# Issuing the first expert's output stores from ScalarE instead of SyncE

## The chip, the cores and the metric

The kernel runs on one core of a Trainium2 chip. The metric is the device time of one launch, in microseconds (us). Before the change it is 1227.88 us, the median of three runs (1226.94 to 1229.16).

## What is computed

The reference chains three blocks in fp32:

```python
scores = scale * np.matmul(q, k.transpose(0, 1, 3, 2))     # 4 x 8 heads, 576 x 576, head width 64
kth = np.partition(scores, -32, axis=-1)[..., -32:-31]     # the 32nd largest of each row
scores = np.where(scores >= kth, scores, -1e9)
attn = softmax(scores);  x = attn @ v                      # 2304 tokens x 512
g = x @ w_gate;  x = (silu(g) * (x @ w_val)) @ w_out       # first expert, inner width 1536
h = x @ w_in;    out = (h * np.cos(h)) @ w_out             # second expert, inner width 2048
```

## The kernel before

**Tiling.** The 2304 tokens are 18 tiles of 128. They are worked through in ten chunks: two of one tile, then eight of two tiles. For each chunk, each of four head pairs, each tile and each head there is one unit of attention (144 in all): TensorE makes the scores in PSUM (L591 or L598), ScalarE copies them to SBUF (L603), VectorE finds the 32 largest with four MAX8 (L628) and three MATCH_REPLACE8 (L631), ScalarE makes the masked exponentials (L659, L670), TensorE transposes them (L692), ScalarE fetches the transposed blocks (L698) and TensorE multiplies with V (L745, L748). In between run the matmuls of the first expert of the chunk before: gate and value (L903), with ScalarE fetching from PSUM (L869, L870, L881), GpSimd multiplying, ScalarE rounding the result (L965), and the output matmul (L1070), which sums a tile's output in one of two PSUM banks named y.

**The step that changes.** When a tile's output sum is finished, `y_proc` (L1092) turns it and writes it to the DRAM buffer y1, from which the second expert loads it (L1332). It does so in two halves of 256 columns, 36 halves in all. For each half ScalarE copies the sum to the SBUF tile yo (L1105), TensorE transposes its two 128x128 blocks back into the bank (L1111), ScalarE copies the transposed blocks into the same yo tile (L1116), and a DMA stores the tile, 128 KB, to y1 (L1117). There is one yo buffer (`r_yo` is a ring of one), so the copy L1105 of the next half waits until the store before it has landed. The bank is free for the next tile after the second half's copy.

**Queues and order.** The program is laid out ahead of time by a small planner (`Plan`, L90): every step is a generator item with an engine, a planned cost and a due time, the planner runs the items in planned time, and each item's function appends its instructions to the engines' queues at that moment. On the chip every engine then runs its own queue strictly in order and waits on semaphores. A DMA stands in the queue of the engine that issues it. Before the change all DMAs but two at the very start (L465) are issued by SyncE (SP): the output weights of the first expert (wo; L376, L378, L380), raw second-expert weights (L357) and their converted form (L361), Q, K and V loads (L490, L515, L542, L544), the stores in question (L1117), the second expert's inputs and weights (L1332, L1247) and its stores (L1576, L1694). A store in SP's queue waits there for ScalarE's copy L1116, and every DMA behind it waits with it. The planner's item that holds the copy and the store is one ScalarE item of 0.27 us planned cost.

**The second expert.** After the attention the second expert runs as two long runs of matmuls: L1407 (input product, in seven products per 2x2 block scheme) and L1684 (output product), with VectorE and ScalarE splitting operands (L1374, L1378, L1290, L1293, L1655, L1659) and making h·cos(h) (L1544 to L1561).

Of the kernel before, what the change touches and what calls it, by code (L numbers as in the profile page):

```python
# [165 lines left out]
def topk_attention_moe_moe(ctx: ExitStack, tc: tile.TileContext, qT, kT, vP, w1, wo1, w2, out):  # L166
    nc = tc.nc
# [4 lines left out]
    y1 = dram.tile([128, KT, NTOK], F32, name="y1")  # L172
# [681 lines left out]
    def moe_due(c, f):  # L854
        return due_unit((FIRST[c] + SIZES[c]) * H) + 20.0 + f * SIZES[c] * H * PACE / NF1
# [236 lines left out]
    def y_proc(c, i):  # L1092
        due = moe_due(c, NF1) - 80.0 * (c >= NCH - 2)
        bank = yt[i % NYB]
        y4 = bank.rearrange("p (f n) -> p f n", f=KT)
        for half in range(2):
            ko = yo_count[0]
            yo_count[0] += 1
            yield r_yo.gate(ko)
            y2 = y4[:, 2 * half:2 * half + 2]  # L1100
            st = {}

            def fetch(y2=y2):
                st["y"] = moe.tile([128, 2, 128], F32, tag="yo", name="yo", bufs=r_yo.n)
                nc.scalar.activation(st["y"], y2, AF.Copy)  # L1105

            yield "ACT", 0.27, fetch, due, True

            def turn(y2=y2):
                for j in range(2):  # L1110
                    nc.tensor.transpose(y2[:, j], st["y"][:, j], ident)  # L1111

            yield "PE", 0.22, turn, due + 2.0, True

            def store(y2=y2, half=half):
                nc.scalar.activation(st["y"], y2, AF.Copy)  # L1116
                nc.sync.dma_start(y1[:, 2 * half:2 * half + 2, i * 128:i * 128 + 128], st["y"])  # L1117

            end = yield "ACT", 0.27, store, due, True
            r_yo.free(ko, end + 2.5, plan)  # L1120
        r_y[i % NYB].free(i // NYB, end, plan)
        ev_y1[i].set(end + 2.5, plan)
# [661 lines left out]
```

## Time and profile before

| what | value |
|---|---|
| median of three runs | 1227.88 us (1226.94 to 1229.16) |
| the profiled execution | 1223.17 us, of which 1221.4 us are the span of its instructions |
| TensorE (PE) busy | 1169.9 us, 96% |
| VectorE (DVE) busy | 1002.2 us, 82% |
| ScalarE (ACT) busy | 937.9 us, 77% |
| GpSimd (POOL) busy | 574.8 us, 47% |
| granted TensorE clock, mean | 0.993 of full speed |
| the DMAs that move | 36 stores of 128 KB, first issue at 166.3 us, last at 853.7 us |

How to read the profile: it is one execution of the program taken by the hardware profiler. An engine is busy while one of its compute instructions runs; issuing a DMA is not busy time. `SPq` or `ACTq` mark what an engine's sequencer does (issue a DMA, wait for an event). L1117 is line 1117 of the kernel. `y<-yo` means that the instruction writes the tensor y and reads the tile yo. Ahead of each wait stands the instruction that waited, behind the arrow what ended its wait. PEld is the weight load that goes ahead of a matmul. Engines overlap the tail of one instruction with the head of the next, so starts can lie closer together than durations.

### The profile page before, as it was taken

What the parts mean: (1) busy time and instruction counts of PE and PEld (TensorE: products, weight loads), DVE (VectorE), ACT (ScalarE), POOL (GpSimd) and SP (SyncE); (2) the same over time, 40 slices, a digit from 0 to 9 for tenths busy, and PEclk for the clock granted to TensorE, in tenths of its full rate; (3) what the DMA queues carried; (4) which work ended last, traced back from release to release, by engine and by line L of the source; (5) the groups of instructions that cost most, each with busy time, mean ns of one, the idle gap of its engine ahead of it and who ended that gap; (6) DMA issues with size and microseconds to landing.
All of it is one profiled execution on the core that took longest, in us unless ns stands there. A gap on an engine that the chain in (4) does not pass through costs nothing. (4 is left out here: it accounts for less than half of the span.)

```text
span 1221.4 us, 23299 instructions
## 1 busy us (share of the span) xinstructions
PE 1169.9 (96%) x7720; PEld 1018.3 (83%) x7720; DVE 1002.2 (82%) x1984; ACT 937.9 (77%) x2085; POOL 574.8 (47%) x1036
## 2 busy tenths in 40 slices
PE   5799979999999999999999999999999999999998
PEld 3577646898888898898988898999999998888887
DVE  7999999999999999999999997277867778644541
ACT  4789999898889989898988887446756678755651
POOL 4898976876687876777766765300000000000000
PEclk9799999999999999999999999999999999999999
DMA  7455556665545653656545533463344276443430
GB/s 260 152 189 169 178 159 195 205 205 184 191 152 165 226 176 123 210 181 202 179 150 187 175 121 102 158 215 124 124 166 136 110 249 199 147 122 104 129 104 27
DMA packets 138985, 199.96 MB, mean 164 GB/s; under 512 B 19312, under 2 KB 88432, under 8 KB 138864
## 3 DMA queue, kind: packets, MB, share of 16 engines
q1 hardware_dynamic: 138704, 198.40, 51.1%
q8 instruction: 61, 1.00, 0.3%
q14 instruction: 60, 0.49, 0.1%
q10 hardware_dynamic: 160, 0.07, 0.0%
HBM read 152.28 MB, written 46.14 MB: 162 GB/s over the span
## 5 line engine op out<-in xcount | busy, mean ns | idle before, releaser
L628 DVE MAX8 m<-w 128x8 f32<-128x576 f32 x432 | 309.5, 747 | 1.8
L903 PE MATMUL gv<-x,w 128*128 128x256 f32 x2016 | 271.2, 286 | 0.3 <-ACT hg L870 0.3
L903 PEld LDWEIGHTS gv<-x,w 128*128 128x128 f32 x2016 | 252.2, 191 | 2.9 <-ACT hg L870 0.9
L631 DVE MATCH_REPLACE8 w<-m,w 128x576 f32<-128x576 f32 x288 | 213.0, 742 | 0.0
L1684 PE MATMUL b<-w2o,gp 128*128 128x512 f32 x864 | 202.1, 396 | 0.0
L1684 PEld LDWEIGHTS b<-w2o,gp 128*128 128x128 f32 x864 | 162.4, 188 | 38.7
L1407 PE MATMUL b<-xc,w 128*128 128x288 f32 x1344 | 182.1, 297 | 2.2 <-DVE h L1472 2.2
L1407 PEld LDWEIGHTS b<-xc,w 128*128 128x128 f32 x1344 | 180.2, 189 | 3.3 <-DVE h L1472 2.7
L1070 PE MATMUL y<-wo,gh 128*128 128x512 f32 x400 | 147.1, 414 | 4.1 <-DMA wo<-wo 1.9
L659 ACT ACTIVATE e<-s,b 128x576 f32<-128x576 f32 x144 | 113.5, 789 | 9.8 <-POOL b L642 9.5
L628 DVE MAX8 m<-s 128x8 f32<-128x576 f32 x144 | 107.2, 745 | 12.8 <-ACT s L603 11.6
L670 ACT ACTIVATE e<-e,b 128x576 f32<-128x576 f32 x144 | 114.1, 793 | 4.2 <-POOL b L646 0.3
L603 ACT ACTIVATE s<-sc 128x576 f32<-128x576 f32 x144 | 95.0, 660 | 20.3 <-PE sc L591 16.2
L698 ACT ACTIVATE pt<-tp 128x512 f32<-128x512 f32 (+1 forms) x216 | 101.4, 498 | 11.3 <-PE tp L692 10.7
L631 DVE MATCH_REPLACE8 w<-m,s 128x576 f32<-128x576 f32 x144 | 106.9, 742 | 0.0
L692 PE MATMUL tp<-ident,e 128*128 128x128 f32 x648 | 98.3, 275 | 8.8 <-ACT e L670 3.6
L1070 PEld LDWEIGHTS y<-wo,gh 128*128 128x128 f32 x400 | 75.0, 189 | 26.2 <-issue 4.0
L598 PE MATMUL sc<-K,q 128*128 128x288 f32 (+1 forms) x512 | 92.1, 307 | 3.9 <-ACT s L603 3.6
L692 PEld LDWEIGHTS tp<-ident,e 128*128 128x128 f32 x648 | 77.7, 141 | 19.7 <-ACT pt L698 5.5
L1070 PE MATMUL y<-wo,gl 128*128 128x512 f32 x208 | 84.8, 414 | 3.8 <-POOL wo L249 3.5
L598 PEld LDWEIGHTS sc<-K,q 128*128 128x128 f32 (+1 forms) x512 | 73.4, 183 | 10.8 <-ACT s L603 5.8
L748 PE MATMUL av<-pt,V 128*64 128x256 f32 (+3 forms) x832 | 75.2, 324 | 0.0
(115 smaller groups left out, 2081.6 us busy)
## 6 DMA issues: line engine op xcount, KB each, us to landing
wo<-wo SPq DMA_DIRECT2D x96, 512.0 KB, 3.6
gr<-gd SPq DMA_DIRECT2D x72, 256.0 KB, 3.2
w_raw<-in_w SPq DMA_DIRECT2D x32, 511.8 KB, 4.5
V<-in_vP SPq DMA_DIRECT2D x52, 256.0 KB, 3.0
w<-in_w SPq DMA_DIRECT2D x24, 511.5 KB, 5.7
kx<-in_kT SPq DMA_DIRECT2D x64, 144.0 KB, 3.0
wo<-wo SPq DMA_DIRECT2D x36, 256.0 KB, 3.0
gd<-h SPq DMA_DIRECT2D x32, 288.0 KB, 2.1
```

Source lines behind the costliest of these rows:

```text
L598: nc.tensor.matmul(sc[:r1, s, :HALF], q[:, a, (t - t0) * 128:(t - t0) * 128 + r1], k[:, s * HALF:s * HALF + HALF], start=a == 0, stop=a == 1)
L603: nc.scalar.activation(st["s"], sc[:, :, :HALF], AF.Copy)
L628: nc.vector.max(out=st["m"][:, 8 * i:8 * i + 8], in_=st["w"] if i else st["s"])
L631: nc.vector.match_replace(out=st["w"], in_to_replace=st["m"][:, 8 * i:8 * i + 8], in_values=st["w"] if i else st["s"], imm_value=LOWEST)
L659: nc.scalar.activation(st["e"], st["s"], AF.Prelu, bias=st["b"][:, 1:2], scale=SCALE, alpha=STEEP)
L670: nc.scalar.activation(st["e"], st["e"], AF.Exp, bias=st["b"][:, 2:3], scale=1.0, accum_out=smT[c, p, g][:, j:j + 1])
L692: nc.tensor.transpose(st["ps"][:, j - j0], e[:, j * 128:j * 128 + 128], ident)
L698: nc.scalar.activation(pt[:, j0:j1], st["ps"][:, :j1 - j0], AF.Copy)
L903: nc.tensor.matmul(gv[g], W1[f, kk // 2][:, a, g, kk % 2], m, start=kk == 0 and i == 0, stop=kk == KT - 1 and i == 2)
L1070: nc.tensor.matmul(bank, m, w, start=f == 0 and n == 0, stop=f == NF1 - 1 and n == len(terms) - 1)
L1407: nc.tensor.matmul(ps[b], w[:, a, side, kk], x[:, e, kk], start=start and kk == 0 and m == 0, stop=kk == 1 and m == 2, skip_group_check=True)
L1684: nc.tensor.matmul(st["o"], g[:, a, cs], W2O[f][:, b], start=f == 0 and i == 0, stop=f == NF2 - 1 and i == 2)
```

## The change

The DMA that stores a half of a tile's output is put in ScalarE's queue, directly behind the copy that fills its source, and no longer in SyncE's. Nothing else differs: the copy, the buffers, the planned costs and the order of all other instructions are the same.

```diff
             def store(y2=y2, half=half):
                 nc.scalar.activation(st["y"], y2, AF.Copy)
-                nc.sync.dma_start(y1[:, 2 * half:2 * half + 2, i * 128:i * 128 + 128], st["y"])
+                nc.scalar.dma_start(y1[:, 2 * half:2 * half + 2, i * 128:i * 128 + 128], st["y"])
 
             end = yield "ACT", 0.27, store, due, True
             r_yo.free(ko, end + 2.5, plan)
```

## Rows read from the trace of the kernel before

**Rows 1.** The page, part 1: busy time, share of the span, instructions.
```profile
span 1221.4 us, 23299 instructions
...
PE 1169.9 (96%) x7720; PEld 1018.3 (83%) x7720; DVE 1002.2 (82%) x1984; ACT 937.9 (77%) x2085; POOL 574.8 (47%) x1036
```

**Rows 2.** The chain that ended last, in order of time: start us, us, what.
```profile
853.21 10.50 PE b L1407 x78
...
882.36 132.26 PE b L1407 x990
...
1019.02 198.81 PE b L1684 x852
```

**Rows 3.** Busy us of each engine in the stretches that hold the stores.
```profile
core 0: us, PE busy (x) PEld busy (x) DVE busy (x) ACT busy (x) POOL busy (x), PEclk, DMA share, GB/s
160.00:210.00 50.00, 42.65 (x234) 29.09 (x235) 47.48 (x95) 45.61 (x105) 32.22 (x51) 0.97 0.59 178
285.00:308.00 23.00, 21.23 (x155) 18.34 (x153) 23.00 (x51) 20.59 (x53) 15.31 (x31) 1.00 0.47 142
373.00:397.00 24.00, 23.95 (x197) 22.39 (x197) 21.35 (x44) 23.40 (x62) 18.26 (x34) 1.00 0.47 143
458.00:483.00 25.00, 25.00 (x192) 23.01 (x191) 25.00 (x55) 24.56 (x64) 15.15 (x31) 1.00 0.33 99
534.00:560.00 26.00, 25.43 (x204) 22.95 (x201) 24.84 (x52) 23.93 (x61) 20.40 (x36) 1.00 0.56 174
620.00:648.00 28.00, 27.11 (x205) 24.77 (x204) 27.62 (x58) 25.30 (x65) 19.25 (x40) 1.00 0.53 163
700.00:728.00 28.00, 28.00 (x210) 25.38 (x207) 27.66 (x57) 23.02 (x62) 19.79 (x41) 1.00 0.37 115
780.00:800.00 20.00, 20.00 (x158) 19.50 (x157) 11.65 (x22) 11.17 (x26) 0.00 (x0) 1.00 0.61 195
835.00:856.00 21.00, 20.82 (x152) 20.24 (x152) 14.78 (x28) 15.41 (x32) 0.00 (x0) 1.00 0.34 108
```

**Rows 4.** The tile yo: duration ns min/median/max, first and last start, waits, landing.
```profile
L1105 ACT ACTIVATE yo<-y x36: 363/386/537, 164.6 to 851.0; 128x256 f32<-128x256 f32 x36
L1116 ACT ACTIVATE yo<-y x36: 361/386/507, 165.9 to 853.3; 128x256 f32<-128x256 f32 x36
L1117 SPq DMA_DIRECT2D y<-yo x36: 360/371/663, 166.3 to 853.7; - x36
...
DMA to landing us min/median/max: 1.8/1.9/3.8
```

**Rows 5.** Waits: of SP's queue at the stores; of the engines around them.
```profile
SPq L1117 <- ACT yo L1116: 56.8, 20, 5.5
...
PEld y L1111 <- ACT yo L1105: 5.8, 11, 1.1
...
ACT yo L1105 <- DMA y<-yo: 5.2, 6, 1.4
...
PE y L1111 <- ACT yo L1105: 2.7, 6, 0.9
```

**Rows 6.** ScalarE's timeline around one store: start us, us, instruction [idle before].
```profile
627.75 0.38 ACT L1116 ACTIVATE yo<-y 128x256 f32<-128x256 f32 x1
628.01 0.66 ACT L603 ACTIVATE s<-sc 128x576 f32<-128x576 f32 x1
...
632.04 0.38 ACT L1105 ACTIVATE yo<-y 128x256 f32<-128x256 f32 x1 [1.19 <-DMA y<-yo]
```

**Rows 7.** The line L465, issued by both queues at the program's start: ns min/median/max.
```profile
L465 SPq DMA_DIRECT2D qr<-in_qT x8: 465/570/1435, 3.1 to 17.9; - x8
L465 ACTq DMA_DIRECT2D qr<-in_qT x2: 547/627/707, 0.9 to 1.5; - x2
```

**Rows 8.** SP's timeline at the first stores, and the matmul that waits on SP's load.
```profile
163.76 1.29 SPq L515 DMA_DIRECT2D qx<-in_qT  x2
166.27 0.38 SPq L1117 DMA_DIRECT2D y<-yo  x1
166.75 5.10 SPq L376 DMA_DIRECT2D wo<-wo  x3
...
169.47 2.03 PE L1070 MATMUL y<-wo,xw 128*128 128x512 f32 x2 [2.33 <-DMA wo<-wo]
```

## The prediction

> **What bounds the kernel now.** I read the busy times first: TensorE is busy 1169.9 of 1221.4 us, ScalarE 937.9 [rows 1]. Busy time is only an average, so next comes the chain that ended last. From 882.36 us on it is nearly nothing but TensorE: 132.26 us of L1407 and 198.81 us of L1684 in one piece each, and before that a piece of 10.50 us from 853.21 [rows 2]. The last store is issued at 853.7 [rows 4]. So the last third of the kernel holds no store and runs at TensorE's pace; the change can only move the moment at which that third begins. Third, the stretches that hold the stores, seven of 23 to 50 us with four stores each between 160 and 728 us and two later ones with four each [rows 3]. From 373 us on the reader sees TensorE without slack there (23.95 of 24, 25.00 of 25, 25.43 of 26, 27.11 of 28, 28.00 of 28 us), VectorE hardly looser, and ScalarE, the engine that gets the new work, 23.40 of 24 and 24.56 of 25 us busy in two of them. Between 160 and 210 TensorE has room (42.65 of 50) and VectorE sets the pace (47.48). Last, the waits: SP stands 56.8 us in 20 waits at the stores for their copy, while the weight load of the transpose waits 11 times in 36 for ScalarE's copy L1105 [rows 5]. A copy that comes later still therefore meets a TensorE that is already waiting for it.
>
> **What is removed.** SP loses 36 issues at a median of 371 ns, 13.4 us [rows 4], and the waits at the stores [rows 5]. SP computes nothing, and its time counts only where a load behind a store is late and an engine waits for it. The clearest case: at 169.47 TensorE waits 2.33 us for a wo load that SP issued at 166.75, right behind the store of 166.27; the issue before that one ended at 163.76 + 1.29 = 165.05 [rows 8]. Freed of the store, the load could go out up to 166.27 - 165.05 = 1.2 us sooner. I take 0 of it: TensorE idles 7.35 us of those 50 us [rows 3] anyway, and VectorE, the nearer bound there, doesn't wait for this product. If that cover is not real it is a gain of 1.2 us.
>
> **What is added.** ScalarE runs in order. Today the instruction behind the copy starts 628.01 - 627.75 = 0.26 us after the copy's start, while the copy still runs [rows 6]. With the store behind it, the queue must first wait until yo is written (0.38 us), then issue the DMA, and only then pass on the next instruction. SP takes 0.371 us for the issue [rows 4]. ScalarE issuing this store is not in the trace; on the one line that both queues issue, ScalarE takes a median of 627 ns against SP's 570, 1.10 times as long [rows 7], so I take 0.41 us. The price of a store is then 0.38 + 0.41 - 0.26 = 0.53, with some 20 ns between copy and issue 0.55 us. Below it lies 0, if issuing held nothing up; above it 0.38 + 0.707 + 0.02 - 0.26 = 0.85 us with ScalarE's longest issue [rows 7]. I take 0.55, since the 371 ns are of this very transfer. In sum 36 x 0.55 = 19.8 us of ScalarE's queue.
>
> Queued behind the waiting store on ScalarE are the score copies (L603) that VectorE waits for, the fetches that free TensorE's banks (L698, L869, L870, L881) and the next L1105. The price is hidden where ScalarE would have idled before anyone misses its result. Four stores cost 4 x 0.55 = 2.2 us a stretch. ScalarE's idle time in the seven stretches is 4.39, 2.41, 0.60, 0.44, 2.07, 2.70 and 4.98 us [rows 3]. In four of them it covers the 2.2 us; in the other three it falls short by 1.60, 1.76 and 0.13, together 3.5 us. There ScalarE ends the stretch late, and as TensorE is 98 to 100% busy in these it has no idle time in which to catch up what it loses. In the two stretches after 780 us ScalarE idles 8.83 of 20 and 5.59 of 21 us, so the eight stores there cost 0; if that cover fails, 8 x 0.55 = 4.4 us. A count from the other side: TensorE's load already waits for L1105 in 11 transposes, and six L1105 themselves wait for a landing [rows 5], a wait that swallows the price of the store before; so 5 to 11 transposes are hit at 0.55 us, 2.8 to 6.1 us. The 3.5 lies within. With the price 0.85 the same subtraction gives shortfalls of 0.99, 2.80, 2.96, 1.33 and 0.70 us, 8.8 us; with the price 0 it gives 0.
>
> **The landing.** The next half's L1105 waits for the landing of the store before it in six cases, 5.2 us together, 1.19 of them at 632.04 [rows 5, 6]; a store lands 1.8 to 3.8 us after its issue, median 1.9 [rows 4]. The trace has no store of this kind on a queue of its own. Bounds: unchanged, or all 5.2 us gone; a slower landing, by the 0.04 us of the longer issue, is too small to count. I take unchanged, as the median is close to the minimum already. Beside it the Trainium skill, in the page "DMA: Bandwidth & Descriptors", section "Issuing engines are not separate DMA queues", says that transfers started by several engines share the same 16 DMA engines and that only the sequencer's issue time is saved, usually small beside the transfer. By that rule the landing is unchanged and the change saves no more than SP's issue time, which stands on no path here; it speaks against a gain.
>
> **The sum.** -0 (SP) + 3.5 (ScalarE) - 0 (landing) = +3.5 us: the profiled execution of 1223.17 us would become 1226.7. That execution lies 4.7 us below the median of the runs, 1227.88, so I put the difference on the median: 1231.4 us. About 0.2% (2.5 us) is what a measurement of this kernel can tell from no change.
>
> **Rivals.** *Hidden.* ScalarE's late 0.55 us never reaches TensorE, because what TensorE takes from it lies ready in the other buffers. For it: in the 458 to 483 stretch ScalarE idles only 0.44 us and yet TensorE is 25.00 of 25 us busy [rows 3], so it doesn't live from hand to mouth. Against it: the 11 waits for L1105 [rows 5]. Time: 1227.9.
>
> *Faster: the landing.* SP's loads are large, and a store that is queued behind one lands late; from ScalarE's own queue it need not. Its place is the wait of L1105 for the landing. It decides once those landings fall from up to 3.8 us to about the 1.8 of the fastest and so give back more than the new price takes. Worth: TensorE waited 2.7 us in all for L1105, ScalarE 5.2 [rows 5], so 2.7 to 5.2; with the price hidden, and 4 us taken between the two, 1223.9. Against it: only six of 36 copies waited so, and every one of the 36 stores pays. Beside it the same page, section "Queues, rings and completion order", says that each DMA engine goes round between the queue rows it has work for, packet by packet; by it a store would overtake loads that are queued on SP's row, which is this rival.
>
> *Heavy.* Every late microsecond stays, because each engine is kept busy by the one before: 19.8 us, 1247.7. For it: in the four stretches from 373 to 648 us TensorE, VectorE and ScalarE are all busy 89% or more [rows 3]. Against it: the idle time of ScalarE within the same rows, and the hold-up of at most 0.55 us at a time.
>
> **How the numbers follow.** The forecast (a part of the price reaches TensorE, 0 to +8.8 us, likeliest +3.5) gets 0.43, hidden 0.27, faster by the landing 0.18, heavy 0.12. The likeliest time is 1231.4. The range goes from 1224.5, which takes in hidden and the weaker half of the faster rival, to 1241, the forecast with its dearer price and the beginning of the heavy case; outside lie about 0.1 on each side. Slower by over 0.2%: heavy 0.12 and 0.38 of the forecast, 0.50. Within 0.2%: hidden, and the forecast's low end, 0.32. Faster: 0.18. The likeliest case's own range is 1228 to 1237.
>
> **What would show it.** In the profile after, the stores stand under ScalarE's queue, and the instruction behind a copy L1116 starts about 0.26 + 0.55 = 0.8 us after the copy's start; 0.26 again would mean no price, over 1.1 a dearer one. SP's waits at L1117 are gone; whether its time turns into earlier loads shows at the 2.33 us wait for wo. The wait of L1111 for L1105 grows from 2.7 us if the forecast holds and shrinks if the landing wins. ScalarE's wait for the landing, 5.2 us, should stay near its size less the price that it swallows; near 0 with landings all at 1.8 speaks for the faster rival. The long run of L1407, which began at 882.36, begins some 3.5 us later. The prediction is wrong if that run begins at the same time or sooner, or over 9 us later.

## The result and the profile after

| what | before | after |
|---|---|---|
| median of five runs each | 1227.88 us (1226.94 to 1229.16) | 1239.57 us (1238.24 to 1242.06) |
| ratio, 95% interval | | 1.0089 [1.0071, 1.0108]: slower |
| the profiled execution / its span | 1223.17 / 1221.4 us | 1238.24 / 1236.5 us |

The kernel got slower, by 0.9%, or 11.7 us between the medians. The forecast had the sign and 3.5 us. (The kernel before was run five times too; the table ahead of the prediction says three. The ratios here and below are the record's own and needn't equal the quotient of two medians; where a figure in us comes from a ratio, the text says so.) The two profiled executions lie 15.1 us apart, because the one of before is 4.7 us below its median; below, a position in one execution is read against a position in the same execution wherever it can be.

First the busy times of after (its page, part 1), the lines that answer to [rows 1]. No engine runs more instructions than before. Of the 15.1 us TensorE idles 9.6; its 7720 matmuls are also busy 5.5 us longer (1175.4 against 1169.9), of which some 1.9 are found in the tail, below, and the rest wasn't followed up.

```profile
span 1236.5 us, 23270 instructions
...
PE 1175.4 (95%) x7720; PEld 1019.9 (82%) x7720; DVE 1003.4 (81%) x1984; ACT 939.1 (76%) x2085; POOL 573.7 (46%) x1036
```

The chain that ended last (start us, us, what), against [rows 2]. The long piece of L1407 begins at 897.43, where before it began at 882.36: all 15.1 us are lost before it, and its own 132.27 us are as before. Two landings of stores now stand in the chain, at 791.63 and 805.05, where before there was one (2.62 us, at 791.38).

```profile
791.63 6.11 DMA y<-yo
...
805.05 3.03 DMA y<-yo
...
897.43 132.27 PE b L1407 x990
```

The tile yo of after, as in [rows 4]. The stores are in ScalarE's queue (ACTq), their issue takes 366 ns, and the slowest landing has gone from 3.8 to 6.1 us.

```profile
L1105 ACT ACTIVATE yo<-y x36: 362/386/425, 164.7 to 866.6; 128x256 f32<-128x256 f32 x36
L1116 ACT ACTIVATE yo<-y x36: 363/387/445, 165.9 to 868.5; 128x256 f32<-128x256 f32 x36
L1117 ACTq DMA_DIRECT2D y<-yo x36: 366/366/400, 166.4 to 868.9; - x36
...
DMA to landing us min/median/max: 1.8/2.1/6.1
```

The waits of after (sum us, times, longest). SP's line of 56.8 us at L1117 [rows 5] is gone. TensorE's waits for the copy L1105 have grown, 5.8 to 13.8 us for its weight load and 2.7 to 8.9 for its matmul; ScalarE's for a landing from 5.2 to 8.2. TensorE's longest single wait of each kind is about three times that of before.

```profile
PEld y L1111 <- ACT yo L1105: 13.8, 14, 3.0
...
PE y L1111 <- ACT yo L1105: 8.9, 12, 2.8
...
ACT yo L1105 <- DMA y<-yo: 8.2, 6, 3.8
```

ScalarE's timeline at one store (start us, us, instruction, [idle before it]), against [rows 6]. The next instruction, L603, starts 636.64 - 635.82 = 0.82 us after the copy, where before it was 0.26: the price of a store is 0.56 us here, and 0.55 to 0.68 at the others (next starts 0.81 to 0.94 after the copy's), but for one of 0.86; the mean of the next starts is 0.86, so the mean price 0.60. The trace itself says why: 0.44 us idle, ended by the copy whose end the store waited for, with the issue of 0.37 us in that gap.

```profile
635.82 0.38 ACT L1116 ACTIVATE yo<-y 128x256 f32<-128x256 f32 x1
636.23 0.37 ACTq L1117 DMA_DIRECT2D y<-yo  x1
636.64 0.65 ACT L603 ACTIVATE s<-sc 128x576 f32<-128x576 f32 x1 [0.44 <-ACT yo L1116]
```

**Where the time went.** Busy time of each engine from 20 to 780 us and from 780 to 815, of before and then of after; columns as in [rows 3]. By 780 us TensorE has done 5062 matmuls instead of 5116. The gap grows fastest behind that: in the 35 us that follow, 214 instead of 253, with 3.6 us of TensorE idle and the clock granted at 0.95, where before it was busy 34.73 of 35 us.

```profile
20.00:780.00 760.00, 723.29 (x5116) 620.70 (x5117) 716.77 (x1481) 661.78 (x1575) 569.10 (x1017) 0.99 0.55 173
780.00:815.00 35.00, 34.73 (x253) 32.84 (x252) 23.40 (x47) 16.55 (x38) 0.00 (x0) 1.00 0.72 236
```

```profile
20.00:780.00 760.00, 717.99 (x5062) 614.26 (x5063) 718.33 (x1481) 659.50 (x1566) 562.14 (x1009) 0.99 0.54 172
780.00:815.00 35.00, 31.36 (x214) 27.86 (x213) 12.01 (x23) 14.70 (x35) 5.82 (x9) 0.95 0.45 141
```

Store by store, the copy L1116 of after runs later than the same copy of before by 2.5 us at the fifth store, 3.2 at the 12th, 5.2 in the stretch of 458 us, 7 to 8.5 in that of 534, some 8 through the two after it, 9.3 at the 29th, 14.0 at the 32nd and 15.2 at the last. So there are two losses of different kinds: a slow one over 28 stores, and 4.7 us within three stores. How late one execution is by the 29th store says little about its size: e8 below, which is the kernel before up to there, is 5.3 us late at that store in its own execution. The slow loss is therefore taken from medians. From the 29th to the 32nd store that same execution loses 0.3 us, so a loss of 4.7 us over these three stands out.

The second, in lines. ScalarE and TensorE of after behind the 29th store: it is issued at 791.63, lands 6.11 us later, ScalarE stands 3.83 us for its buffer, and TensorE 2.78 us for ScalarE.

```profile
791.22 0.38 ACT L1116 ACTIVATE yo<-y 128x256 f32<-128x256 f32 x1 [2.02 <-PE y L1111]
791.63 0.37 ACTq L1117 DMA_DIRECT2D y<-yo  x1
...
797.76 0.38 ACT L1105 ACTIVATE yo<-y 128x256 f32<-128x256 f32 x1 [3.83 <-DMA y<-yo]
```

```profile
798.20 0.69 PE L1111 MATMUL y<-ident,yo 128*128 128x128 f32 x2 [2.78 <-ACT yo L1105]
```

The wait isn't all of the 4.7 us. Between the copies of the 29th and the 32nd store (columns as in [rows 3]; before, then after) TensorE idles 2.78 us and is busy 1.93 us longer, for nearly as many matmuls (126 on the trace against 123), and the clock granted is 0.91. After the wait it was 0.50, the lower of its two levels (1.2 GHz), from 798 to 800 us, 0.68 in the next 2 us and 1.00 from 802 on; a run of 36 matmuls of L903 that took 4.55 us before the wait (from 790.88) takes 5.78 behind it (from 798.54).

```profile
781.90:796.25 14.35, 14.35 (x123) 14.35 (x122) 8.63 (x17) 7.79 (x19) 0.00 (x0) 1.00 0.65 203
791.20:810.26 19.06, 16.28 (x126) 16.08 (x125) 8.43 (x17) 8.07 (x19) 0.00 (x0) 0.91 0.49 152
```

SP's timeline around the same store, before and then after. Before, SP issued nothing from 780.14 (779.21 + 0.93) until the store, and wo, xr and two wr went out behind it. After, SP doesn't stand there: wo, xr and wr (512, 288 and twice 128 KB) go out from 789.54 on, 0.1 us behind the loads ahead of them and in the 2 us ahead of the store.

```profile
779.21 0.93 SPq L1247 DMA_DIRECT2D wr<-w2d  x2
782.32 0.37 SPq L1117 DMA_DIRECT2D y<-yo  x1
782.79 0.41 SPq L380 DMA_DIRECT2D wo<-wo  x1
783.25 0.45 SPq L1332 DMA_DIRECT2D xr<-y  x1
783.74 0.94 SPq L1247 DMA_DIRECT2D wr<-w2d  x2
```

```profile
788.51 0.93 SPq L1247 DMA_DIRECT2D wr<-w2d  x2
789.54 0.38 SPq L380 DMA_DIRECT2D wo<-wo  x1
789.96 0.43 SPq L1332 DMA_DIRECT2D xr<-y  x1
790.44 1.10 SPq L1247 DMA_DIRECT2D wr<-w2d  x2
792.03 0.37 SPq L1332 DMA_DIRECT2D xr<-y  x1
```

The DMA queues of after (packets, MB, share of 16 engines) in 791 to 793 us, 793 to 795 and 795 to 798: q1 is SP's, q10 ScalarE's. From its issue at 791.63 until 795 the store moves no packet, while SP's loads hold the engines 92.6 and 98.4% of the time.

```profile
q1 hardware_dynamic: 386, 0.47, 92.6%
...
q1 hardware_dynamic: 419, 0.71, 98.4%
...
q1 hardware_dynamic: 675, 0.66, 62.4%
q10 hardware_dynamic: 272, 0.13, 14.7%
```

### The profile page after: what moved, and what is told of

Read it like the earlier page. It is cut to its first block, busy times and chain, and to the rows that moved or that the text cites. A ratio compares the mean times of both kernels' runs of the same rounds, so it can differ in the third digit from the quotient of the medians.

```text
span 1236.5 us, 23270 instructions
## 1 busy us (share of the span) xinstructions
PE 1175.4 (95%) x7720; PEld 1019.9 (82%) x7720; DVE 1003.4 (81%) x1984; ACT 939.1 (76%) x2085; POOL 573.7 (46%) x1036
## 5 line engine op out<-in xcount | busy, mean ns | idle before, releaser
L903 PE MATMUL gv<-x,w 128*128 128x256 f32 x2016 | 271.4, 286 | 0.1
L903 PEld LDWEIGHTS gv<-x,w 128*128 128x128 f32 x2016 | 252.2, 191 | 2.8 <-ACT hg L870 1.1
L1407 PE MATMUL b<-xc,w 128*128 128x288 f32 x1344 | 182.3, 297 | 2.6 <-DVE h L1472 2.2
L1407 PEld LDWEIGHTS b<-xc,w 128*128 128x128 f32 x1344 | 180.2, 189 | 3.9 <-DVE h L1472 2.7
L1070 PE MATMUL y<-wo,gh 128*128 128x512 f32 x400 | 147.0, 413 | 4.2 <-DMA wo<-wo 3.9
L603 ACT ACTIVATE s<-sc 128x576 f32<-128x576 f32 x144 | 93.9, 652 | 23.6 <-PE sc L591 16.3
L1070 PEld LDWEIGHTS y<-wo,gh 128*128 128x128 f32 x400 | 74.9, 189 | 25.9 <-issue 3.9
L1070 PE MATMUL y<-wo,gl 128*128 128x512 f32 x208 | 85.6, 418 | 3.6 <-POOL wo L249 3.1
L969 POOL TENSOR_TENSOR gl<-vv,gh 128x256 fp32r<-128x256 f32 x84 | 61.9, 738 | 30.0 <-ACT gh L965 23.8
```

Of the source, the lines that this page charges most:

```text
L603: nc.scalar.activation(st["s"], sc[:, :, :HALF], AF.Copy)
L903: nc.tensor.matmul(gv[g], W1[f, kk // 2][:, a, g, kk % 2], m, start=kk == 0 and i == 0, stop=kk == KT - 1 and i == 2)
L1070: nc.tensor.matmul(bank, m, w, start=f == 0 and n == 0, stop=f == NF1 - 1 and n == len(terms) - 1)
L1407: nc.tensor.matmul(ps[b], w[:, a, side, kk], x[:, e, kk], start=start and kk == 0 and m == 0, stop=kk == 1 and m == 2, skip_group_check=True)
```

## The experiments

Theory: two costs, the hold of ScalarE's queue (0.55 us a store) and, in the tail, the store that now stands behind SP's loads. Rivals: the hold is all of it; or the move is all of it and the hold is hidden. "Late" is always against the copy L1116 of the same number in the profile of before. The code cuts are shortened: they show the lines that matter, some of them broken in two.

**e1_hold: the hold alone.** The kernel before, with three copies of one column behind the copy, each on itself, so that ScalarE is held about as long. The store stays with SP.

```diff
                 nc.sync.dma_start(y1[:, 2 * half:2 * half + 2, i * 128:i * 128 + 128], st["y"])
+                [nc.scalar.activation(halfpi, halfpi, AF.Copy) for _ in range(3)]
```

> The kernel of before, its stores still on SyncE, with three copies of a 128x1 constant onto itself put behind each copy L1116, which hold ScalarE's queue for some 0.5 us more and do nothing else. Theory (the 0.57 us by which a store holds ScalarE's queue makes the 9.3 us that are lost by the 29th store): +6 to +9 us, 1234 to 1237, and no loss in the stretch after 780 us beyond 1 us. Rival (the loss comes from SyncE's queue running differently once the stores are gone, not from ScalarE): within 2 us of before, 1226 to 1230.

Measured: 1236.27 us against 1229.46, ratio 1.0064 [1.0042, 1.0085]. The size of the hold is right (below, ScalarE's timeline): the next instruction starts 0.83 us after the copy's start, as with the store in the queue. It costs 6.8 us between the medians, 7.9 by the ratio. Between the 29th and the 32nd store nothing is lost (17.6 to 17.9 us late in that execution) and no landing takes over 3.0 us there. So the hold by itself makes a loss of 0.4 to 0.85%, and the loss of the tail isn't the hold.

```profile
492.37 0.43 ACT L1116 ACTIVATE yo<-y 128x256 f32<-128x256 f32 x1
492.63 0.72 ACT L1117 ACTIVATE halfpi<-halfpi 128x1 f32<-128x1 f32 x3
493.26 0.75 ACT L698 ACTIVATE pt<-tp 128x512 f32<-128x512 f32 x2
```

**e2_behind: the move with most of the hold taken away.** The changed kernel, but the store is kept back and put into ScalarE's queue behind the next step of ScalarE that the planner places.

```diff
-                nc.scalar.dma_start(y1[:, 2 * half:2 * half + 2, i * 128:i * 128 + 128], st["y"])
+                plan.held.append(lambda y=st["y"], half=half: nc.scalar.dma_start(
+                    y1[:, 2 * half:2 * half + 2, i * 128:i * 128 + 128], y))
...
-            fn()
+            held, self.held = self.held, [] if engine == "ACT" else self.held
+            fn(); [f() for f in held if engine == "ACT"]
```

> The changed kernel, with each store put behind the next ScalarE step instead of directly behind its copy, so that waiting and issuing can run while that step computes. Theory: the hold falls from 0.57 us to under 0.2, the 29th store is late by at most 3 us instead of 9.3, the slow landings after 780 us stay (some 4 us): 1229 to 1234. Rival (it is the issue itself, 0.37 us, that holds the engine, wherever it stands): the hold stays at 0.4 us or more, the 29th store is late by 6 us or more: 1235 to 1239.

Measured: 1232.74 us, 1.0029 [1.0013, 1.0046]. In ScalarE's timeline the next instruction starts 0.26 us after the copy again, and most of the store's issue lies under it. The instruction after that one can still be held: below, L869 starts 0.61 us after L881, just as the issue ends, where before it was 0.26. So the hold is smaller here, not gone. Set against the kernel before, the second instruction starts 0.17 us later on the mean of the 31 stores where the same instructions follow (0.57 in the changed kernel): 0.24 to 0.47 us in 13 of them, whose covering instruction is short, 0.6 at one, and 0.12 or less at the rest.

```profile
552.84 0.40 ACT L1116 ACTIVATE yo<-y 128x256 f32<-128x256 f32 x1
553.10 0.41 ACT L881 ACTIVATE vv<-gv 128x256 f32<-128x256 f32 x1
553.27 0.39 ACTq L1117 DMA_DIRECT2D y<-yo  x1
553.71 0.39 ACT L869 ACTIVATE th<-gv 128x256 f32<-128x256 f32 x1 [0.20 <-POOL b L646]
```

The same two instructions in the kernel before:

```profile
550.76 0.43 ACT L881 ACTIVATE vv<-gv 128x256 f32<-128x256 f32 x1
551.02 0.44 ACT L869 ACTIVATE th<-gv 128x256 f32<-128x256 f32 x1
```

The 29th store is only 2.5 us late, and the loss of the tail is there: 6.5 us late at the 32nd, 8.6 at the 33rd. The waits of this kernel from 782 to 870 us show the same 6.4 us for landings as the changed kernel has in that stretch (6.4, 4 times, longest 3.8):

```profile
ACT yo L1105 <- DMA y<-yo: 6.4, 4, 4.0
```

The two halves add up within their intervals: 1.0064 for the hold and 1.0029 for the move make 1.0093, against 1.0089 for both. As a rest of the hold is in the second, they overlap a little.

**e4_tail_sp: SP's queue for the last eight stores.** The changed kernel, with the stores of the last two chunks back in SP's queue.

```diff
-                nc.scalar.dma_start(y1[:, 2 * half:2 * half + 2, i * 128:i * 128 + 128], st["y"])
+                (nc.sync if c >= NCH - 2 else nc.scalar).dma_start(
+                    y1[:, 2 * half:2 * half + 2, i * 128:i * 128 + 128], st["y"])
```

> The changed kernel, with the eight stores after 780 us back on SyncE and the first 28 on ScalarE. Theory: the 9.3 us before 782 us stay and the 5.8 us after it go, in the median 1233 to 1236, with landings there at most 2.7 us. Rival (every one of the 36 stores costs the same share of the whole, 11.7/36 = 0.32 us): 8 x 0.32 = 2.6 us come back, 1237.

Measured: 1235.88 us, 1.0054 [1.0036, 1.0071]. The 29th store is 10.0 us late and the last one 10.3, and landings from 780 to 822 us take 1.8 to 3.1 us. SP's timeline shows the order of before again, store first and loads behind it:

```profile
792.36 0.37 SPq L1117 DMA_DIRECT2D y<-yo  x1
792.83 0.41 SPq L380 DMA_DIRECT2D wo<-wo  x1
793.28 0.45 SPq L1332 DMA_DIRECT2D xr<-y  x1
```

So the loss of the tail hangs on which queue holds the store there.

**e3_stands: SP stands, but doesn't store.** The changed kernel, with a DMA of one column of yo (512 bytes, 4 a partition) behind each store in SP's queue, so that SP waits where it waited and ScalarE stores. This was to show whether the standing alone puts the loads back.

```diff
                 nc.scalar.dma_start(y1[:, 2 * half:2 * half + 2, i * 128:i * 128 + 128], st["y"])
+                nc.sync.dma_start(stand, st["y"][:, 0, :1])
```

> The changed kernel, with a store of one column of the same tile (512 bytes) to a scratch buffer issued by SyncE at the old place, so that SyncE's queue stands there for the copy again and its loads can't run ahead. Theory (the landings of up to 6.1 us after 780 us come from loads that SyncE issues ahead of the store): those landings fall to 3 us or less, 3 to 5 us come back: 1234.5 to 1236.5. Rival (a transfer from ScalarE's queue is served later by itself): landings of 3.6 to 6.1 us stay, 1238.5 to 1241.

Measured: 1462.03 us, 1.1903 [1.1859, 1.1946]. That answers nothing about the question. The DMA issues (KB each, median us to landing) show that the tiny store is itself slow, 8.5 us, and takes the 128 KB store beside it from 2.1 to 9.7; ScalarE then waits 157.8 us for its buffer.

```profile
y<-yo ACTq DMA_DIRECT2D x36, 128.0 KB, 9.7
...
stand<-yo SPq DMA_DIRECT2D x36, 0.5 KB, 8.5
```

**e5_halves: the same question with no tiny row.** The store is cut into two of 64 KB, one in each queue.

```diff
-                nc.scalar.dma_start(y1[:, 2 * half:2 * half + 2, i * 128:i * 128 + 128], st["y"])
+                [q.dma_start(y1[:, 2 * half + b, i * 128:i * 128 + 128], st["y"][:, b])
+                 for b, q in enumerate((nc.scalar, nc.sync))]
```

> The changed kernel, with each store cut into two DMAs of 64 KB: the first 128 columns are stored by ScalarE, the second by SyncE at the old place, so that SyncE's queue stands there for the copy again while ScalarE still waits and issues. Theory (the landings of up to 6.1 us after 780 us come from loads that SyncE issues ahead of the store): both halves of the stores there land within 3.2 us, the time lost between the 29th store and the last falls from 5.9 to under 1.5 us, the hold of 0.57 us stays: 1234 to 1237. Rival (a transfer on ScalarE's queue is served late by itself): ScalarE's halves still land after 3.6 to 6.1 us there, 1238.5 to 1242.

Measured: 1240.03 us against 1229.00, 1.0077 [1.0055, 1.0099]. SP stands again and issues its half before wo (796.54, then 796.96), landings from 780 to 822 us take at most 3.1 us, also those in ScalarE's queue, and between the 29th and the 32nd store only 0.5 us are lost (14.2 to 14.7). So it isn't ScalarE's queue that is slow; it is SP's loads going out ahead. The time as a whole missed its expectation all the same: the execution is 14.2 us late by the 29th store already (the changed kernel's was 9.3 and e1's 17.6, single executions all three), which fits a slow loss as large as with the whole store in ScalarE's queue, and a landing of 3.85 us at the 35th comes on top. Nor does the interval of the time part it from the changed kernel's.

**e6_two_tail and f3_two_turn: a second buffer in the tail.** If a late landing costs only because L1105 waits for the one yo buffer, a second one should cover it. Both are the changed kernel with the space of another tile, hg, as second buffer in the last two chunks: e6 takes it for every second half of a tile, f3 for every second copy in the order of the halves (ko).

```diff
-                tag="yo", name="yo", bufs=r_yo.n)
+                tag="hg" if c >= NCH - 2 and half else "yo", name="yo", bufs=r_yo.n)    # e6
+                tag="hg" if c >= NCH - 2 and ko % 2 else "yo", name="yo", bufs=r_yo.n)  # f3
```

> The changed kernel with a second buffer for yo in the last four tiles only (their second halves take the space of hg, which nothing uses by then), so that the copy of a half needn't wait for the landing of the half before it. Theory (after 780 us the loss is the wait of L1105 for late landings): the late landings stay, L1105's waits there fall from 6.4 to 2 us or less, 3 to 5 us come back: 1234.5 to 1236.5. Rival (the loss after 780 us is ScalarE's held queue): 1238.5 to 1241.

> The changed kernel with yo alternating between two buffers in the order in which the halves are worked (the run before alternated by half, but the halves of two tiles are interleaved, so it took away one wait of three). Theory (after 780 us the loss is the wait of L1105 for late landings): its waits for a landing there go to under 1 us, the time lost between the 29th store and the 32nd falls from 4.7 to under 1 us, 1.0089 falls to about 1.005. Rival (other transfers that are late because SyncE's loads run ahead hold the same engines): waits elsewhere take their place, 1.008 or more.

Measured: e6 1238.02 us, 1.0068 [1.0047, 1.0089]. The halves of two tiles alternate in the tail, so that two in a row still took the same buffer: 4.6 us of waits for landings stay, and no gain shows. f3: 1236.36 us against 1229.55, 1.0061 [1.0037, 1.0085]. The landings stay late, but ScalarE's waits for them from 782 to 870 us fall from 6.4 us to one of 1.6, and from the 29th to the 32nd store 0.9 us are lost (14.2 to 15.1) instead of 4.7. Another 3.1 us are lost behind the 32nd (15.1 to 18.2; 1.2 in the changed kernel, 1.7 in f2, whose stores are all SP's, 0.9 in e8). The time, 1.0061, lies between the 1.005 expected and the rival's 1.008, and its interval takes in both: the waits bear the theory out, the time alone doesn't.

**e8_before_two_tail: what that buffer is worth to the kernel before.** The edit of e6 on the kernel before.

> The kernel of before (all stores on SyncE) with the second yo buffer in the last four tiles. Theory: L1105's three waits for a landing after 780 us, 2.3 us together, go, but TensorE is 20.00 of 20 us busy there and hardly waits for these copies: 0 to 1.5 us faster, 1226.5 to 1229. Rival (those waits stand on the path): 2 us or more faster.

Measured: 1228.46 us, 0.9996 [0.9984, 1.0008]. It is worth nothing there, so e6 doesn't gain from room that the kernel before lacked as well. f3's order of the two buffers wasn't tried on the kernel before.

**f1_hold_slack and f2_hold_full: where the hold costs.** e1's hold, but only at the 16 stores of the four stretches in which the prediction had ScalarE's idle time cover it (f1), or only at the 12 of the three in which it fell short (f2). The cuts are against e1.

```diff
-                [nc.scalar.activation(halfpi, halfpi, AF.Copy) for _ in range(3)]
+                [nc.scalar.activation(halfpi, halfpi, AF.Copy) for _ in range(3) if ko < 8 or 20 <= ko < 28]  # f1
+                [nc.scalar.activation(halfpi, halfpi, AF.Copy) for _ in range(3) if 8 <= ko < 20]             # f2
```

> The kernel of before with ScalarE's queue held (the three small copies, 0.6 us) only at the 16 stores of the four stretches in which the prediction found ScalarE's idle time to cover four stores (160 to 210, 285 to 308, 620 to 648 and 700 to 728 us). The prediction's subtraction: 0 us, ratio within 0.1% of 1. Rival (every hold costs about the same, 6.8 us for 36 of them): 16 x 0.19 = 3.0 us, ratio 1.0025.

> The same hold only at the 12 stores of the three stretches in which ScalarE's idle time falls short (373 to 397, 458 to 483, 534 to 560 us). The prediction's subtraction with 0.6 us: 1.8 + 2.0 + 0.3 = 4.1 us, ratio 1.0033. Rival (every hold costs about the same): 12 x 0.19 = 2.3 us, ratio 1.0018. If holds cost their full 0.6 us where TensorE has no room: 7.2 us, ratio 1.006.

Measured: f1 1231.49 us, 1.0021 [1.0003, 1.0039], or 2.6 us by the ratio (0.4 to 4.8); f2 1233.21 us, 1.0029 [1.0012, 1.0046], or 3.6 us (1.5 to 5.7), both against 1229.55. Together they make 6.2 us for 28 holds, as much for each as e1's 7.9 for 36. The stretches with little idle time cost more for each hold (0.30 us against 0.16), but the intervals overlap, so that this difference isn't shown. The ones with enough idle time don't cost nothing, though the interval ends close to it.

**e7_behind_tail_sp and f4_behind_two_turn: both costs taken away.** e7 is e2 with the last eight stores in SP's queue; f4 is e2 with the second buffer of f3, all stores in ScalarE's queue.

```diff
-                plan.held.append(lambda y=st["y"], half=half: nc.scalar.dma_start(
+                (plan.held.append if c < NCH - 2 else lambda f: f())(lambda y=st["y"], half=half: (
+                    nc.scalar if c < NCH - 2 else nc.sync).dma_start(                                # e7
```

> Both remedies: the first 28 stores on ScalarE behind the next ScalarE step, the last eight on SyncE as before. Theory (hold and late landings are all of the loss, and they add): within 0.2% of before, about 1228 to 1231. Rival (something else is lost as well when stores go by ScalarE's queue): 1232 or more.

> The changed kernel with the store behind the next ScalarE step and the two buffers of yo in the last four tiles, all stores on ScalarE. Theory (hold and landing waits are the loss): 1.0029 of the first remedy alone falls to between 0.999 and 1.0015. Rival (SyncE's loads running ahead cost something else too): 1.002 or more.

Measured: e7 1231.37 us, 1.0017 [1.0003, 1.0031], of which 2 us stay unexplained; f4 1228.31 us, 1.0003 [0.9982, 1.0023], as the kernel before. The interval of f4 ends well below that of the changed kernel; it doesn't part f4 from e7 or e2. In f4 landings of up to 6.5 us stay in the tail, but ScalarE waits 0.7 us for one, once. With most of the hold hidden and the late landing covered, no loss shows any more, and no gain either: no version beats the kernel before.

## Why the prediction was right in sign and short in size

**The price of a store: right.** The step gave 0.55 us, made of the copy's remainder, the issue and a gap. Measured were 0.55 to 0.68 and once 0.86, 0.60 on the mean, with the issue at 0.366 us instead of 0.41. The view of the tile yo names who pays it: among those who waited for it are now ScalarE's own score copies and fetches (below), which before were not in that list.

```profile
  ACT s L603: 2.5, 5
  ACT pt L698: 2.2, 5
  ACT vv L881: 2.2, 5
```

**"In the other three it falls short", 3.5 us: the size fits.** f2 holds ScalarE in these three stretches alone and costs 3.6 us. Its interval (1.5 to 5.7) also takes in the 2.3 us of its rival, that every hold costs the same, so the subtraction behind the 3.5 isn't shown.

**"In four of them it covers the 2.2 us", 0 us: this step failed.** f1 puts the hold there alone and loses 2.6 us (0.4 to 4.8). A likely reason, argued and not tested: idle time summed over a stretch was set against a price summed over it, but a hold comes at one moment, and ScalarE's idle time elsewhere in the 23 to 50 us doesn't serve the engine that waits right then. Over all 36 stores e1 puts the part of the price that reaches the end at 6.8 us (7.9 by the ratio) of 21.8 (36 holds of 0.61, the mean in its trace), about a third.

**"A slower landing ... is too small to count" and "the eight stores there cost 0": this failed, and it is the larger error.** I looked at the longer issue only, and at SP's stores as something that is held up by SP's loads. It is the other way round: while the store stood in SP's queue, the loads behind it stood too, and the store went first. Taken out, it lets SP run ahead; at 791.63 it meets 1 MB that was issued since 789.54, and lands after 6.11 us. With one yo buffer that stalls ScalarE and then TensorE, and TensorE's clock is granted lower behind its wait: 4.7 us from the 29th to the 32nd store, 2.8 idle and 1.9 longer busy. e1 excludes the hold for it; e2 keeps it with most of the hold gone; e4 removes it by the queue alone, and e5 by the order, with half of each store still in ScalarE's queue. The bounds that I put on the landing ran from unchanged to a gain and had no loss in them.

The terms as measured, f2 3.6, f1 2.6 and 4.7 for the tail, sum to 10.9 us; measured are 10.9 by the ratio (0.0089 x 1227.88) and 11.7 by the medians. That they agree to a tenth is luck: the first two are each known to some 2 us, the third is from one execution, and the hold of the last eight stores isn't in the sum.

**The SP term, 0: nothing speaks against it.** SP's 13.4 us of issues and 56.8 us of standing turned into longer waits for others (below, the waits of SP's queue after; the first, at the loads of wo for the matmuls that still read their buffers, was 85.6 us before, the second, at the loads of L542, 74.5). The longest wait of L1070 for a wo load fell from 2.3 to 1.4 us, by 0.9 of the 1.2 that the step named as its bound. Such waits of its matmuls as a whole didn't fall (4.3 us before, 4.5 after); those of its weight loads did, from 5.6 to 3.0. No run was made to price this.

```profile
SPq L380 <- PE y L1070: 107.5, 42, 12.3
SPq L542 <- PE av L748: 93.9, 24, 15.4
```

**The rivals.** *Hidden* is excluded by e1's interval. *Faster by the landing*: the median landing went from 1.9 to 2.1 us, and at the 29th store q10 moved nothing for 3.4 us. By the section "Queues, rings and completion order" of the Trainium skill's page "DMA: Bandwidth & Descriptors" each DMA engine serves in turn the queue rows that it has work for, packet by packet. From 795 us on the trace agrees: q10's packets run among q1's (170 and 302 in the first us). For the 3.4 us before, with q1 at 92.6 and 98.4%, it shows no such turns; whether q10's row had work for the engines by then, and what made the store wait, isn't shown. *Heavy* (19.8 us) is off by a factor of three in e1.

**What I said would show it.** The next instruction 0.8 us after the copy: 0.82. SP's waits at L1117 gone: yes. The wait of L1111 grows: from 2.7 to 8.9 us. The landing's 5.2 us stays: no, 8.2, and that is the line that speaks of the second cost. The long run over 9 us later was my mark for a wrong prediction; it began 15.1 us later in that execution, so by its own test the size was wrong. The medians, 11.7 us apart, stay inside the range of 1224.5 to 1241, but outside the 1228 to 1237 of the likeliest case. That is partly luck: the upper end was put there for a dearer price of a store and the beginning of *heavy*, and neither came; what filled that room was the late landing, for which the sum had no loss.

## What to carry to other kernels

A DMA put right behind the instruction that writes its source costs an in-order compute queue the rest of that instruction plus the issue, here 0.6 us for 128 KB, of which about a third reached the end; placed one instruction later, most of that is hidden, all of it where the covering instruction is long. A queue that stands at a store also holds back the loads behind it: before moving the store, look at what will go out earlier, and whether the store's buffer can bear a landing behind it. Compare a price with the idle time at its own moment, not with a sum over the stretch.

## What was not expected of the hardware

A store of 4 bytes from each of 128 partitions (512 bytes in all) took 8.5 us to land at the median, longer than any of the 128 KB stores in the changed kernel (1.8 to 6.1 us), and slowed the 128 KB store from the same tile to 9.7 us (e3). And a store in a queue of its own, with nothing ahead of it in that queue, moved its first packet 3.4 us after its issue at 791.63, while another queue's loads kept the DMA engines 92.6 and 98.4% busy.
